# Attention feeding an MLP on one core: q and k transposed by DMA, 4-token sums on GpSimd, v loaded twice, in a new order

## The chip, the core and the metric

The kernel runs on one core of a Trainium2 chip. The metric is device time in microseconds (us) of one execution; less is better. A run is called slow when it is over 1.5% above the fastest of the same kernel. The times in us are medians of all runs; the ratios leave the slow ones out. A ratio is always the mean time of one kernel's fast runs over the mean time of the fast runs of the kernel before in the same rounds on the same chip, so it is not quite the ratio of the medians that stand beside it. The brackets after a ratio are its 95% interval.

Engines: PE is TensorE, PEld its weight load, ACT is ScalarE, DVE is VectorE, POOL is GpSimd, SP is SyncE, whose queue (SPq) issues nearly all DMA here. "The rings" are the 16 DMA engines that serve all queues.

## The reference

There are 8 batches of 8 heads, 576 tokens, 64 dimensions. Every batch does two attentions: a local one (each token sees 3 tokens to each side) and a global one over means of 4 tokens (144 of them). Their sum, as a 4608 x 512 matrix, goes through an MLP with 2048 hidden units.

```python
q_d, k_d, v_d = (t.reshape(B, H, 144, 4, D).mean(axis=3) for t in (q, k, v))
out_up    = np.repeat(softmax_attention(q_d, k_d, v_d), 4, axis=2)
out_local = softmax_attention(q, k, v, mask=np.abs(pos[:, None] - pos[None, :]) < 4)
x   = (out_up + out_local).transpose(0, 2, 1, 3).reshape(4608, 512)
h   = x @ w_in                                     # 512 x 2048
out = np.where(h > 0, h, np.exp(np.minimum(h, 0)) - 1) @ w_out    # 2048 x 512
```

Inputs and output are fp32; the kernel computes in fp16.

## The kernel before

The work on one batch is four head pairs (b, j). For each pair, q, k and v are loaded with 96 tokens on partitions (k and v with 3 halo rows to each side), cast to fp16 on GpSimd, and turned round by matmuls. QI is the identity with four-token averaging columns beside it, so the same matmul yields q transposed and its 4-token means; VR averages v.

```python
def load(b, j):                       # cut: shapes of the access patterns
    nc.sync.dma_start(out=q32[:], in_=rows(q, 0, NB, 0, QB))
    for src, dst in ((k, k32), (v, v32)):
        nc.sync.dma_start(out=dst[0:96], in_=rows(src, 0, NB, 0, QB))
        for c0, nblk, tok, p in ((lo, NB - lo, -3, 96), (0, hi, QB, 99)):
            ...                       # 2 loads of 3 halo rows each

def transposes(b, j):
    tq, tk = two("tq"), two("tk")     # PSUM
    for c in range(NB):               # q: transposed, and its 4-token means
        nc.tensor.matmul(tq[:, ...], q16[:, c, :, :], QI[:], start=True, stop=True)
    for c in range(NB):               # v: 4-token means
        nc.tensor.matmul(tq[0:KG, ...], VR[:, ...], v16[:, c, :, :], ...)
    nc.scalar.copy(out=qt[:], in_=tq[...])
    nc.vector.tensor_copy(out=vd[:], in_=tq[0:KG, ...])
    for c in range(NB):               # k, as q
        nc.tensor.matmul(tk[:, ...], k16[:, c, :, :], KI[:], start=True, stop=True)
    nc.scalar.copy(out=kt[:], in_=...); nc.vector.tensor_copy(out=kd[:], in_=...)
```

Then follow scores, exponentials, denominators ("den"), a broadcast of the reciprocals ("rd" to DRAM and "rcb" back), outputs ("lg"), and on GpSimd the sum of local and global part ("xt"), which is the MLP's input. The MLP has 9 blocks of 512 tokens: mm1 (tile hp, 16 groups of four matmuls per block), the activation, mm2 (tile op, the same count), and a store of the output (tile os). The whole order is written by hand, in "slots": one slot is one mm1 group and one mm2 group, and attention's pieces are put at slot numbers between them.

```python
SLOTS = (0, 1.6, 3.2, 4.8, 9.7, 11.3, 12.9, 14.5)     # transposes, scores of 4 pairs
base = start_of(b) - 26.5                             # start_of(b): the mm1 of block b
at(base + slots[2 * j], transposes, b, j)
at(base + slots[2 * j + 1], scores, b, j)
```

The softmax here doesn't subtract the row's maximum and nothing guards it: scores larger than these inputs give would overflow.

## Time and profile before

The median is 406.56 us (405.73 to 407.38, 2 runs). The page of the profiled run, a third one of 403.56 us, cut to the span, PE's busy time, PE and DMA in 40 slices of about 10 us (a digit is a tenth), the load queue (packets, MB, share of 16 rings' span) and the chain of waits that ended last:

```profile
span 401.8 us, 8092 instructions
...
PE 353.0 (88%) x3052; PEld 185.6 (46%) x3052; DVE 254.4 (63%) x460; ACT 203.8 (51%) x377; POOL 138.7 (35%) x184
...
PE   1465688687986899999999999999899899999996
...
DMA  6998999965966980796199639926820310100112
...
q1 hardware_dynamic: 129420, 47.62, 55.0%
...
PE 67%; DMA 12%; POOL 6%; issue 4%; DVE 4%; SPq 3%; ACTq 2%; ACT 1%; POOLq 0%; DVEq 0%
```

PE is full from the 15th slice on, and the chain is two thirds PE. The table of stretches of the same run shows for each window the length, the busy time of the engines, the granted PE clock, the share of the rings and GB/s:

```profile
core 0: us, PE busy (x) PEld busy (x) DVE busy (x) ACT busy (x) POOL busy (x), PEclk, DMA share, GB/s
...
124.00:145.00 21.00, 15.57 (x152) 8.05 (x151) 15.57 (x31) 10.04 (x18) 10.39 (x15) 0.84 0.99 188
...
165.00:203.00 38.00, 37.98 (x367) 20.21 (x366) 30.19 (x55) 24.04 (x46) 14.44 (x20) 1.00 0.67 142
203.00:241.00 38.00, 37.88 (x366) 20.07 (x365) 29.40 (x54) 23.71 (x45) 15.17 (x21) 1.00 0.74 147
```

PE is busy 37.98 of 38.00 us, at full clock.

The first denominator matmuls of a batch are a good mark for the pace. In the timeline of PE (start, length, instruction), those of batch 3 and of batch 7 stand here:

```profile
155.19 0.30 PE L240 MATMUL den<-SEED 2*32 2x288 f16 x4
...
306.08 0.30 PE L240 MATMUL den<-SEED 2*32 2x288 f16 x4
```

So four batches take 306.08 - 155.19 = 150.9 us, 37.7 us each ("the period" below is always this quarter, from batch 3 to batch 7). Each period is read from one profiled run, and single batches of a run differ; a difference of 1 us between two kernels is not clear. The time splits into a start-up of 155.2 us, a steady part of 150.9 us, and a tail of 95.7 us.

What the change is after is this piece of the timeline:

```profile
177.13 0.48 PE L171 MATMUL tq<-QI,q_2376 96*128 96x120 f16 x6
177.45 0.50 PE L176 MATMUL tq<-v_2378,VR 102*72 102x128 f16 x6
177.78 0.49 PE L186 MATMUL tk<-KI,k_2377 102*128 102x126 f16 x6
178.11 1.03 PE L368 MATMUL hp<-xt,WI 128*128 128x512 f16 x4
```

From 177.13 to 178.11 PE turns one pair round: 0.98 us, a third of it for each of q, v and k, 3.9 us per batch.

### The profile page before, as it was taken

What the parts mean: (1) busy time and instruction counts of PE and PEld (TensorE: products, weight loads), DVE (VectorE), ACT (ScalarE), POOL (GpSimd) and SP (SyncE); (2) the same over time, 40 slices, a digit from 0 to 9 for tenths busy, and PEclk for the clock granted to TensorE, in tenths of its full rate; (3) what the DMA queues carried; (4) which work ended last, traced back from release to release, by engine and by line L of the source; (5) the groups of instructions that cost most, each with busy time, mean ns of one, the idle gap of its engine ahead of it and who ended that gap; (6) DMA issues with size and microseconds to landing.
All of it is one profiled execution on the core that took longest, in us unless ns stands there. A gap on an engine that the chain in (4) does not pass through costs nothing.

```text
span 401.8 us, 8092 instructions
## 1 busy us (share of the span) xinstructions
PE 353.0 (88%) x3052; PEld 185.6 (46%) x3052; DVE 254.4 (63%) x460; ACT 203.8 (51%) x377; POOL 138.7 (35%) x184
## 2 busy tenths in 40 slices
PE   1465688687986899999999999999899899999996
PEld 1352345343553455555545554555454444444442
DVE  0134599732586797697778769886886585555510
ACT  1462157535385376747564855667375334444321
POOL 3365755460850581075028304820450050000000
PEclk9999999968999799999999999999999999999999
DMA  6998999965966980796199639926820310100112
GB/s 121 189 253 258 190 215 234 265 126 134 198 139 130 189 176 16 172 231 125 28 195 217 118 78 194 226 64 121 172 79 33 102 53 28 49 29 28 52 54 78
DMA packets 138082, 53.81 MB, mean 134 GB/s; under 512 B 122580, under 2 KB 131388, under 8 KB 138044
## 3 DMA queue, kind: packets, MB, share of 16 engines
q1 hardware_dynamic: 129420, 47.62, 55.0%
q10 hardware_dynamic: 8624, 5.68, 6.6%
q8 instruction: 24, 0.39, 0.4%
q14 instruction: 14, 0.11, 0.1%
HBM read 43.33 MB, written 9.95 MB: 133 GB/s over the span
## 4 chain that ended last, share of the span: by engine, by line
PE 67%; DMA 12%; POOL 6%; issue 4%; DVE 4%; SPq 3%; ACTq 2%; ACT 1%; POOLq 0%; DVEq 0%
PE op L388 29%; PE hp L368 25%; PE sc L204 2%; PE tk L186 2%; PE tq L176 2%; DVE e L374 2%; PE tq L171 2%; PE lg L325 2%; POOL xt L352 2%; DMA w_170<-in_moe_w_in_dram 2%; DMA rcb<-rd 2%; SPq L149 2%; ACTq L276 2%; DMA w_161<-in_moe_w_in_dram 1%; DMA w_207<-in_moe_w_out_dram 1%
## 5 line engine op out<-in xcount | busy, mean ns | idle before, releaser
L368 PE MATMUL hp<-xt,WI 128*128 128x512 f16 x576 | 150.9, 389 | 4.5 <-DVE gt L377 2.5
L388 PE MATMUL op<-WO,gt 128*128 128x512 f16 x576 | 147.7, 385 | 4.7 <-POOL WO L119 3.8
L373 ACT ACTIVATE e<-hp 128x512 f16<-128x512 f32 x144 | 85.7, 601 | 109.5 <-PE hp L368 90.8
L377 DVE SCALAR_TENSOR_TENSOR gt<-hp,e 128x512 f16<-128x512 f32 x144 | 99.6, 692 | 5.4
L374 DVE TENSOR_SCALAR e<-e 128x512 f16<-128x512 f16 x144 | 63.8, 443 | 51.5 <-ACT e L373 50.5
L368 PEld LDWEIGHTS <-WI 128*128 128x128 f16 x576 | 54.5, 99 | 71.7 <-issue 13.4
L388 PEld LDWEIGHTS <-gt 128*128 128x128 f16 x576 | 54.6, 99 | 68.8 <-issue 7.6
L232 DVE TENSOR_TENSOR mex<-pex,MASK 102x1152 f16<-102x1152 f16 x32 | 29.6, 926 | 40.3 <-ACT pex L222 40.2
L352 POOL TENSOR_TENSOR xt<-ln,gn 128x512 f16<-128x512 f16 (+7 forms) x64 | 42.0, 688 | 34.7 <-DVE ln L343 34.7
L222 ACT ACTIVATE pex<-sc 102x576 f16<-102x576 f32 x64 | 41.4, 647 | 22.3 <-PE sc L214 22.3
L182 ACT CAST qt<-tq 128x720 f16<-128x720 f32 x32 | 24.3, 760 | 30.7 <-PE tq L176 27.3
L394 ACT COPY os<-op 128x512 f32<-128x512 f32 x36 | 21.2, 588 | 25.3 <-PE op L388 25.3
L204 PE MATMUL sc<-qt,kt 64*102 64x96 f16 x384 | 19.1, 226 | 11.5 <-DVE vd L184 6.0
L184 DVE CAST vd<-tq 72x256 f16<-72x256 f32 x32 | 13.2, 413 | 22.3 <-ACT qt L182 22.3
L204 PEld LDWEIGHTS <-kt 64*102 64x102 f16 x384 | 14.4, 135 | 25.8 <-ACT kt L192 12.6
L226 ACT ACTIVATE dex<-sc 72x288 f16<-72x288 f32 x64 | 25.8, 404 | 0.0
L343 DVE TENSOR_TENSOR ln<-lg,rcb 128x576 f16<-128x576 f32 x32 | 23.9, 748 | 0.0
L192 ACT CAST kt<-tk 128x612 f16<-128x612 f32 x32 | 21.8, 680 | 0.1
L176 PEld LDWEIGHTS <-VR 102*72 102x72 f16 x192 | 14.2, 123 | 5.7 <-issue 3.9
L263 DVE RECIPROCAL rc<-den 128x288 f16<-128x288 f32 x8 | 15.6, 1949 | 1.7 <-PE den L257 1.7
L340 DVE TENSOR_TENSOR gn<-lg,rcb 128x144 f16<-128x144 f32 x32 | 9.6, 301 | 5.7 <-POOL xt L352 3.0
L194 DVE CAST kd<-tk 128x144 f16<-128x144 f32 x32 | 9.6, 300 | 1.7 <-ACT kt L192 0.5
(361 smaller groups left out, 265.7 us busy)
## 6 DMA issues: line engine op xcount, KB each, us to landing
out_dram<-os SPq DMA_DIRECT2D x36, 256.0 KB
rcb<-rd ACTq DMA_DIRECT2D x14, 288.0 KB
rcb<-rd ACTq DMA_DIRECT2D x14, 72.0 KB
w_149<-in_moe_w_in_dram SPq DMA_DIRECT2D x1, 512.0 KB
w_152<-in_moe_w_in_dram SPq DMA_DIRECT2D x1, 512.0 KB
w_155<-in_moe_w_in_dram SPq DMA_DIRECT2D x1, 512.0 KB
w_158<-in_moe_w_in_dram SPq DMA_DIRECT2D x1, 512.0 KB
w_161<-in_moe_w_in_dram SPq DMA_DIRECT2D x1, 512.0 KB
```

The lines of the kernel that those rows point to most:

```text
L182: nc.scalar.copy(out=qt[:], in_=tq[:, :, 0 : 3 * QW])
L204: nc.tensor.matmul(sc[e][0:KW, c // 3, QB * (c % 3) : QB * (c % 3) + QB], kt[r, c // 3, c % 3, :], qt[r, c // 3, QW * (c % 3) : QW * (c % ...
L222: nc.scalar.activation(out=pex[:, e, :].rearrange("p (g u) -> p g u", g=2), in_=sc[e][0:KW, :, 0:HB], func=AF.Exp, scale=SCALE,)
L226: nc.scalar.activation(out=dex[:, e], in_=sc[e][0:KG, :, HB : HB + SD], func=AF.Exp, scale=SCALE,)
L232: nc.vector.tensor_tensor(out=mex[:], in0=pex[:], in1=mk2, op=AB.mult)
L343: nc.vector.tensor_tensor(out=ln[:].rearrange("p (g u) -> p g u", g=2), in0=lg[:, :, 0:HB], in1=rcb[:, j, 0:S].rearrange("p (g u) -> p g u ...
L352: nc.gpsimd.tensor_tensor(out=xt(t)[:, j, t0 - TBLK * t : t1 - TBLK * t], in0=ln[:, a:z], in1=_rep4(gn[:, a // 4 : z // 4]), op=AB.add,)
L368: nc.tensor.matmul(hp[:], WI[:, dc, 128 * fc : 128 * fc + 128], x[:, dc, :], start=(dc == 0), stop=(dc == DMC - 1),)
L373: nc.scalar.activation(out=e[:], in_=hp[:], func=AF.Exp)
L374: nc.vector.tensor_scalar(out=e[:], in0=e[:], scalar1=1.0, scalar2=-1.0, op0=AB.min, op1=AB.add)
L377: nc.vector.scalar_tensor_tensor(out=gts[t][:, fc, :], in0=hp[:], scalar=0.0, op0=AB.max, in1=e[:], op1=AB.add)
L388: nc.tensor.matmul(op_[:], gts[t][:, fc, 128 * tt : 128 * tt + 128], WO[:, fc, :], start=(fc == 0), stop=(fc == FCN - 1),)
```

## The change

The intent is to take those 18 matmuls per pair off the full engine, in batches 2 to 7. q and k are transposed by DMA from fp16 tiles; their 4-token sums are formed on GpSimd; v is loaded a second time with 4 tokens in one partition row, so that its sums are two GpSimd additions. (Sums replace means: the exponential's scale and an indicator of 4.0 take up the factors.) With it comes a new order: batch 1's attention runs within the first mm1, every later mm1 is paired with the mm2 of the block before, and a batch's four pairs stand close together. The core of the diff:

```diff
+DMA_T = 2
+    def load_v4(b, j):                        # 288 KB, 72 rows of 4 x 1 KB
+        nc.sync.dma_start(
+            out=w32[0:KG].rearrange("p (x y) -> p x y", x=4),
+            in_=bass.AP(..., ap=[[4 * D, KG], [HB * D, 4], [1, 4 * D]]))
     def cast(b, j):
+        if b >= DMA_T:
+            cq = ck = nc.scalar.copy          # was GpSimd
+    def transposes_dma(b, j):
+        nc.sync.dma_start_transpose(out=kt[:, KP : KP + S].rearrange(...), in_=k16[:].rearrange(...))
+        nc.sync.dma_start_transpose(out=qt[:].rearrange(...), in_=q16[:].rearrange(...))
+    def sums(b, j):
+        nc.gpsimd.tensor_tensor(out=vh, in0=vh, in1=vp[:, :, :, 2:4], op=AB.add)
+        nc.gpsimd.tensor_tensor(out=vd[:]..., in0=vh[:, :, :, 0], in1=vh[:, :, :, 1], op=AB.add)
+        for src, name in ((kt[:, KP : KP + S], "kdd"), (qt[:], "qdd")):
+            nc.gpsimd.tensor_tensor(out=h[:], in0=src[:, 0:S:2], in1=src[:, 1:S:2], op=AB.add)
+            nc.gpsimd.tensor_tensor(out=d[:], in0=h[:, 0:HB:2], in1=h[:, 1:HB:2], op=AB.add)
 ...                                           # v: one load of 112 rows, no halo loads
-    SLOTS = (0, 1.6, 3.2, 4.8, 9.7, 11.3, 12.9, 14.5)
+            base, slots = 16 * (b - 2), (None, -1.5, None, 0.5, None, 2.5, None, 4.5)
+            dens, spread, outs = ((6.5, range(4)),), None, (12.5, 13.7)
+            if dma:
+                at(at_s - 5, load_v4, b, j)
+                at(at_s - 4.9, transposes_dma, b, j)
+                at(at_s - 3, sums, b, j)
 ...                                           # batches 1 and 2: reciprocals spread on PE
```

## The prediction

> **What bounds the kernel now.** From about 145 us on, TensorE: in the table of stretches PE is busy 37.98 of 38.00 us at 165:203, and nearly so at 203:241 and 241:279. One batch of attention takes a period of about 37.6 us there: 128 MLP matmuls at 0.216 us (chain: 0.86 us per four) are 27.6 us, attention is the other 10 us. Of these the transposing matmuls tq, vd and tk take 0.98 us per pair (timeline, 177.13 to 178.11), 3.9 us per batch. Before 145 us PE is not the limit: only 203 of 1152 MLP matmuls (44 us of work) are done. Loads (DMA share 0.9 to 1.2), weight casts (chain: WI and WO waits until 82 us) and the reciprocals' round trip through DRAM (chain: rd 2.1 us, rcb 6.5 us, at 122 to 132 us) set the pace, and mm2 of block 0 runs alone.
>
> **What the change does.** (1) It takes 18 matmuls per pair from PE in batches 2 to 7: 24 x 0.98 = 23.5 us, plus their PSUM copies (ACT 0.76 + 0.68, DVE 0.41 + 0.30 us per pair). (2) q and k casts go from GpSimd to ACT, about the time ACT saves. (3) GpSimd gets six sums per pair; from the xt additions (512 columns 1064 ns, 256: 629, 128: 410) I estimate 3.9 us per pair, 4.7 with the v cast; per batch about 19 plus 5.3 us of xt additions, against 15 now. (4) DMA gets 1.2 MB of v and 1.2 MB of transposes per batch on top of about 5.4 MB. The Trainium skill, "Advanced Engine Details and Errata", X-Bar Transpose, says such transposes are as fast as regular DMAs; no trace here shows one yet. (5) The instruction order shows a new schedule too: batch 1 runs inside mm1 of block 0, every later mm1 is paired with the previous mm2, batches 1 and 2 spread reciprocals on PE, halo loads vanish.
>
> **How much is critical.** Start-up: weights and batches 0 to 2 are still some 19 MB, so I expect mm2 of block 0 to wait for WO until about 85 us; then PE should fill near 90 us instead of 145. That is the larger gain. Steady: PE needs about 33.7 us per batch, but GpSimd's order is sums j0, xt, v cast, sums j1, xt: the last xt, which releases the next mm1, sits behind about 12 us of work that starts only when transposes land. I expect PE to wait 2 to 5 us per batch there: a period of 36 to 38 us, near the old one. The Trainium skill, "GPSIMD Engine Reference", Specifications, says GpSimd shares SBUF interfaces with VectorE; the trace agrees: operation e takes 0.29 us at 345:383, where GpSimd is idle, and 0.47 at 165:203. More GpSimd work means more of that.
>
> Sum: first full period ends near 121 us, five of 37, then 72 us of MLP without attention: about 378 us.
>
> **Predicted:** 378 us, 8 in 10 within 357 to 402. Faster by over 2%: 0.82; within 2%: 0.12; slower by over 2%: 0.06.
>
> **Right or wrong in the profile.** Right: hp and op alternate from about 90 us; tq and tk gone after batch 1; PE waits led by hp for POOL xt and sc for POOL kdd or qdd; GpSimd busy near 190 us; transposes land in 2 to 4 us; period 36 to 38 us.
>
> **What would make it wrong.** Transposes by DMA far slower than copies, or stuck in the one SP queue (waits of SP: loads already wait up to 12.3 us for rd): then scores stall in each batch and it loses. Or GpSimd's sums hide fully: period 34 us, total near 358.

## The result, and the profile after

The changed kernel takes 442.37 us (441.23 to 443.51, 2 runs) against 406.56: ratio 1.0881 [1.0727, 1.1035]. It is slower by 9%. The same lines of its page, and q10, ScalarE's DMA queue:

```profile
span 441.7 us, 7188 instructions
...
PE 354.0 (80%) x2644; PEld 169.5 (38%) x2644; DVE 250.5 (57%) x429; ACT 211.2 (48%) x385; POOL 198.9 (45%) x276
...
PE   2665679819878877876977798889888999999996
...
DMA  9968999786999995999399959996993030101111
...
q1 hardware_dynamic: 166924, 62.16, 74.7%
q10 hardware_dynamic: 6160, 4.06, 5.0%
...
PE 34%; POOL 27%; DMA 16%; issue 6%; SPq 5%; DVE 5%; ACT 3%; ACTq 3%; POOLq 0%; DVEq 0%
```

PE has 408 matmuls fewer, but its busy time did not fall (353.0 to 354.0 us). PE is no longer full before the tail; DMA is at 9 in most slices. In the groups of instructions the mean hp matmul grew from 389 to 402 ns, and the mean granted clock fell from 0.979 to 0.934: PE stops, and after some of the stops it runs at half speed for a few microseconds, so that such a stop costs more than its own length. The Trainium skill, "TensorE: Matmul & The Clock Gate", section "What's actually happening", says the array gets half its clock after an idle window of about 3.4 us; the trace agrees in kind, but not on the length: after the stops of 2.0 us that end at 270.90 and 315.14 us, groups of four op matmuls took 1.71 us instead of 0.86, and after one of 2.7 us that ends at 177.14 they took 0.86. The same stretches as before:

```profile
124.00:145.00 21.00, 16.37 (x144) 7.38 (x146) 12.31 (x22) 11.41 (x23) 12.81 (x20) 0.85 1.24 213
...
165.00:203.00 38.00, 31.96 (x263) 14.77 (x260) 25.89 (x41) 21.50 (x38) 22.13 (x30) 0.96 1.05 168
203.00:241.00 38.00, 29.21 (x229) 13.28 (x228) 20.79 (x36) 17.96 (x32) 17.46 (x26) 0.91 0.92 163
```

PE is busy 29 to 32 of 38 us, and the rings stand at 0.92 to 1.05 instead of 0.67 to 0.74. The marks:

```profile
165.37 0.30 PE L310 MATMUL den<-SEED 2*32 2x288 f16 x4
...
348.18 0.30 PE L310 MATMUL den<-SEED 2*32 2x288 f16 x4
```

| part of the span, us | before | after | difference |
|---|---|---|---|
| start-up, to the mark of batch 3 | 155.2 | 165.4 | +10.2 |
| batches 3 to 7 (four periods) | 150.9 (37.7 each) | 182.8 (45.7 each) | +31.9 |
| tail | 95.7 | 93.5 | -2.2 |

Inside one period, SP's timeline (start, length of issue, instruction) shows a stand and then a burst:

```profile
254.17 10.71 SPq L460 DMA_DIRECT2D out_dram<-os  x2
264.97 0.35 SPq L168 DMA_DIRECT2D vp<-in_v_dram  x1
269.33 1.21 SPq L233 DMA_TRANSPOSE kt_63<-k_3289  x1
...
284.44 2.47 SPq L233 DMA_TRANSPOSE kt_65<-k_3431  x1
```

Two output stores hold the in-order queue until 264.9; at 260 to 264 us the rings are at 0.01. Then the four pairs' loads and transposes follow each other, with the rings at 1.0 to 1.4 from 268 to 300 us. (A share over 1 means that packets overlap; 1.0 is no hard ceiling.) GpSimd's timeline shows it waiting for the second load of v and then working, with no break over 2 us, to 301.7 us (in brackets: idle before, and what ended it):

```profile
269.89 1.35 POOL L248 TENSOR_TENSOR vp<-vp 72x512 f32<-72x512 f32 x1 [14.04 <-DMA vp<-in_v_dram]
...
273.98 0.67 POOL L257 TENSOR_TENSOR hs<-kt_63 128x288 f16<-128x288 f16 x1 [1.95 <-DMA kt_63<-k_3289]
...
286.59 2.64 POOL L416 TENSOR_TENSOR xt<-ln,gn 128x192 f16<-128x192 f16 x4
```

The xt additions that the next mm1 needs stand in the middle of this run. In the waits, three lines tell who waits for what (total, times, longest):

```profile
POOL vp L248 <- DMA vp<-in_v_dram: 61.1, 7, 14.0
...
PE hp L432 <- POOL xt L416: 24.6, 15, 5.7
...
PE sc L282 <- POOL qdd L258: 12.9, 9, 2.7
```

Read alone, these lines accuse GpSimd. The experiments had to tell whether it is the cause or passes the DMA's lateness on.

### The profile page after: what moved, and what is told of

Read it like the earlier page. It is cut to its first block, busy times and chain, and to the rows that moved or that the text cites. A ratio compares the mean times of both kernels' runs of the same rounds, so it can differ in the third digit from the quotient of the medians.

```text
span 441.7 us, 7188 instructions
## 1 busy us (share of the span) xinstructions
PE 354.0 (80%) x2644; PEld 169.5 (38%) x2644; DVE 250.5 (57%) x429; ACT 211.2 (48%) x385; POOL 198.9 (45%) x276
## 3 DMA queue, kind: packets, MB, share of 16 engines
q1 hardware_dynamic: 166924, 62.16, 74.7%
## 4 chain that ended last, share of the span: by engine, by line
PE 34%; POOL 27%; DMA 16%; issue 6%; SPq 5%; DVE 5%; ACT 3%; ACTq 3%; POOLq 0%; DVEq 0%
PE op L452 17%; PE hp L432 15%; POOL xt L416 7%; POOL hs L257 5%; POOL vp L248 4%; POOL vd L249 3%; ACTq L342 3%; POOL kdd L258 2%; DMA vp<-in_v_dram 2%; ACT e L437 2%; DMA w_350<-in_moe_w_in_dram 2%; POOL qdd L258 2%; DMA w_569<-in_moe_w_out_dram 2%; DVE ln L406 2%; DMA w_368<-in_moe_w_in_dram 2%
## 5 line engine op out<-in xcount | busy, mean ns | idle before, releaser
L432 PE MATMUL hp<-xt,WI 128*128 128x512 f16 x576 | 161.8, 402 | 36.0 <-POOL xt L416 24.6
L452 PEld LDWEIGHTS <-gt 128*128 128x128 f16 x576 | 54.9, 101 | 69.5 <-issue 10.7
L248 POOL TENSOR_TENSOR vp<-vp 72x512 f32<-72x512 f32 x24 | 30.6, 1275 | 61.1 <-DMA vp<-in_v_dram 61.1
L416 POOL TENSOR_TENSOR xt<-ln,gn 128x448 f16<-128x448 f16 (+7 forms) x60 | 40.2, 699 | 26.4 <-DVE ln L406 26.4
L249 POOL TENSOR_TENSOR vd<-vp 72x256 f16<-72x256 f32 x24 | 19.9, 831 | 1.9
L282 PE MATMUL sc<-qdd,kdd 64*72 64x144 f16 x96 | 8.1, 245 | 13.2 <-POOL qdd L258 12.9
L328 DVE RECIPROCAL rc<-den 128x288 f16<-128x288 f32 (+1 forms) x9 | 17.6, 1951 | 1.1 <-PE den L310 0.9
L257 POOL TENSOR_TENSOR hs<-qtd 128x288 f16<-128x288 f16 x24 | 16.1, 670 | 1.9
L258 POOL TENSOR_TENSOR kdd<-hs 128x144 f16<-128x144 f16 x24 | 13.6, 567 | 1.9
L258 POOL TENSOR_TENSOR qdd<-hs 128x144 f16<-128x144 f16 x24 | 10.8, 451 | 1.9
L394 PE MATMUL lg<-dex,vd 72*64 72x144 f16 x128 | 10.8, 252 | 0.0
```

Source lines behind the costliest of these rows:

```text
L248: nc.gpsimd.tensor_tensor(out=vh, in0=vh, in1=vp[:, :, :, 2:4], op=AB.add)
L249: nc.gpsimd.tensor_tensor(out=vd[:].rearrange("p g (e d) -> p e g d", e=2), in0=vh[:, :, :, 0], in1=vh[:, :, :, 1], op=AB.add,)
L257: nc.gpsimd.tensor_tensor(out=h[:], in0=src[:, 0:S:2], in1=src[:, 1:S:2], op=AB.add)
L258: nc.gpsimd.tensor_tensor(out=d[:], in0=h[:, 0:HB:2], in1=h[:, 1:HB:2], op=AB.add)
L416: eng.tensor_tensor(out=xt(t)[:, j, t0 - TBLK * t : t1 - TBLK * t], in0=ln[:, a:z], in1=_rep4(gn[:, a // 4 : z // 4]), op=AB.add,)
L432: nc.tensor.matmul(hp[:], WI[:, dc, 128 * fc : 128 * fc + 128], x[:, dc, :], start=(dc == 0), stop=(dc == DMC - 1),)
```

## The experiments

Four theories. **A**: GpSimd's serial run of sums, casts and xt. **B**: the added DMA: it takes time on rings that were not idle in this stage. **C**: ScalarE, which issues the reciprocals' DMAs and stands while it does. **D**: order: the queue stands at output stores while the rings are idle, and the pairs are packed. A further suspect is the transpose itself, slower than a copy. All experiments passed the comparison with the reference. "The changed kernel" below is always the one of the last section: 1.0881, period 45.7.

### e1: all transposes on PE, in the new order

```diff
-DMA_T = 2
+DMA_T = 8
-... (None, -1.5, None, 0.5, None, 2.5, None, 4.5); dens 6.5; outs (12.5, 13.7)
+... (-1.7, -0.5, 0.3, 1.5, 2.3, 3.5, 4.3, 5.5); dens 7.0; outs (12.8, 14.0)
```

> The new schedule, but q and k transposed on PE in all eight batches (no DMA transposes, no GpSimd sums, no second load of v). If the DMA-transpose path (any part of it) is what made the changed kernel slow: the period from one batch's denominators to the next falls from 44 to 47 us to about 38, total 390 to 410 us. If the new schedule itself is at fault: total stays at 430 us or more.

Measured: 419.03 us against 402.0, ratio 1.0407 [1.026, 1.0554]; period 41.0 us, mark of batch 3 at 159.0 us. The new order alone, without any DMA transpose, GpSimd sum or second load, is 4% slower than the kernel before, and its start-up is not shorter (159.0 against 155.2). So less than half of the loss belongs to the order; the DMA path adds the rest: 45.7 - 41.0 = 4.7 us per batch, although it takes 3.9 us per batch off PE.

### e2, e3: doses

e2 adds one GpSimd addition of 128 x 512 per pair; e3 one more 288 KB load of the same rows of v per pair, from batch 3 on, that nobody reads.

```diff
+        nc.gpsimd.tensor_tensor(out=dz[:], in0=qt[:, 0:512], in1=qt[:, 64:576], op=AB.add)   # e2
+        if b > DMA_T:                                                                       # e3
+            nc.sync.dma_start(out=dv[0:KG]..., in_=...)      # as load_v4
```

> The changed kernel with one more GpSimd addition of about 1.06 us per pair (24 in all, result unused). Theory A (GpSimd's serial run of sums is in the loop that sets the period): all of it shows, 4 us per batch, total +20 to +26 us. Theory B (DMA traffic sets the pace) and theory C (ScalarE blocked by issuing rcb DMAs and casts): +0 to +4 us.

> The changed kernel with one more load of 288 KB per pair from batch 3 on (20 loads, 5.9 MB, result unused). Theory B (DMA traffic): about 5.9 MB at 200 GB/s, total +20 to +30 us. Theory A (GpSimd's chain): only a later arrival of the first v tile of a batch, +0 to +8 us. Theory C: no change.

Measured: e2 453.55 us, ratio 1.1264 [1.1104, 1.1424], period 47.8: 2.1 us more per batch for 4.6 us more work (27.8 us for 24 pairs). e3 472.56 us, ratio 1.1736 [1.1543, 1.1929], period 51.5: 5.8 us more per batch for 1.2 MB. By the page, the queue's share times the span is 0.758 x 468.6 = 355 us of ring time against 0.747 x 441.7 = 330 us: 25 us more in five batches, 5 us each. The dose of DMA costs all of its ring time, that of GpSimd about half of its work. Doses show that both lie on the way; they do not say which one binds.

### e4: the sums of q and k on VectorE

```diff
-            nc.gpsimd.tensor_tensor(out=h[:], ...)   # and the next line
+            nc.vector.tensor_tensor(out=h[:], ...)
```

> The changed kernel with the four sums of k and q per pair on VectorE; the two sums of v stay on GpSimd. Theory A: GpSimd's run per batch shrinks by 4 x 2.2 us, the period falls from about 45 to 37 to 40 us, total 400 to 420 us. Theories B and C: within 5 us of the changed kernel (442 us).

Measured: 447.99 us, ratio 1.1126 [1.0983, 1.1269], period 46.3. GpSimd's busy time fell from 198.9 to 146.3 us, 8.8 us per batch, and nothing was gained. The chain of waits by line shows what stands there now:

```profile
PE op L452 20%; PE hp L432 18%; DMA kt<-k 10%; DVE hs L257 4%; DMA w<-in_moe_w_out_dram 4%; DMA w<-in_moe_w_in_dram 4%; ACTq L342 3%; DMA k<-in_k_dram 2%; ACT e L437 2%; DVE gt L441 2%; DVE ln L406 2%; PE sc L274 2%; POOL xt L416 2%; DVE kdd L258 2%; DVE e L438 1%
```

The landing of the k transposes, which does not occur in the changed kernel's chain, has 10% of the span. Theory A alone does not explain the loss. That GpSimd passed the lateness on is the likely reading, but not a proof: the sums went to VectorE, which now has 13% of the chain instead of 5%.

### e5, e6: ScalarE's DMA issues, and everything earlier

e5 spreads the reciprocals on PE in every batch, so ScalarE issues no DMA. e6 puts casts, second load, transposes and loads 3 slots earlier from batch 3 on, and the sums 1.5 slots, with one more buffer of nearly everything.

```diff
-            dens, spread, outs = ((6.5, range(4)),), None, (12.5, 13.7)
+            dens, spread, outs = ((6.5, range(4)),), (8.3, 9.1), (12.5, 13.7)      # e5
-                at(at_s - 5, load_v4, b, j)          # and four more lines like it
+                at(at_s - 5 - early, load_v4, b, j)  # e6: early = 3 if b >= 3
```

> The changed kernel with the reciprocals of every batch spread on PE, as the first three batches have it: no rd and rcb DMAs (0.8 MB per batch) and no 2.6 us of ScalarE issuing them. Theory B (DMA time): period falls by about 4 us, from 45.7 to 41 to 42. Theory C (ScalarE blocked): about the same, 3 to 4 us, but then PE no longer stands still just before the lg matmuls. Theory A (GpSimd): no change in the period, total a little longer by 1.2 us of PE per batch.

> The changed kernel with casts, second v load, DMA transposes and loads of batches 3 to 7 placed 3 slots earlier in program order, sums 1.5 slots earlier; same work, same bytes, one more buffer of k, q and the sums. Theory D (one in-order queue leaves the DMA rings idle for 8 to 9 us per batch while it waits for an output tile): idle time shrinks, period 45.7 to 38 to 42 us, total 15 to 35 us less. Theory B in its pure form (DMA rings simply full): period stays within 1.5 us.

Measured: e5 444.19 us, ratio 1.0986 [1.0809, 1.1163], period 45.6; e6 448.71 us, ratio 1.1098 [1.0948, 1.1248], period 46.1. Neither gains, and issuing earlier did not help. Theory C finds no support. But e5 is a miss for theory B as well. It took the reciprocals' DMA, about 0.8 MB per batch, off the rings: its page has no line for q10. The rings' mean share from the mark of batch 3 to that of batch 7 fell from 0.94 to 0.79, and theory B had expected a period of 41 to 42 us. In exchange PE, which was not full, got 1.2 us of work per batch, by the estimate in the expectation.

### e7: the sums of v on PE, no second load

```diff
-                at(at_s - 5, load_v4, b, j)
-        nc.gpsimd.tensor_tensor(out=vh, ...); nc.gpsimd.tensor_tensor(out=vd[:]..., ...)
+        for c in range(NB):
+            nc.tensor.matmul(vps[0:KG, ...], VR[:, ...], v16[:, c, :, :], ...)
+        nc.vector.tensor_copy(out=vd[:], in_=vps[0:KG, 0:256]...)
```

> The changed kernel with the sums of v made on PE from the fp16 tile as before: no second load of v (1.2 MB per batch, about 5 us of the rings' time), no v sums on GpSimd (8.4 us per batch), 1.3 us more of PE. e4_kq_sums_dve took as much from GpSimd and gained nothing. Theory B: period falls by 4 to 6 us. Theory A: it falls by more than in e4, but only with GpSimd gone from the chain. If neither, within 1 us.

Measured: 423.96 us against 404.79, ratio 1.0486 [1.0351, 1.0621], period 41.95. PE does six matmuls per pair more than in the changed kernel, and the period is 3.75 us shorter. The v part is the bulk of what the DMA path costs: e7 is close to e1 (1.0407) although q and k still go through DMA and GpSimd.

### e8: plain copies instead of transposes

```diff
-        nc.sync.dma_start_transpose(out=kt..., in_=k16...)    # and q
+            nc.sync.dma_start(out=dst[0:96], in_=flat[:, 0:S])
+            nc.sync.dma_start(out=dst[96:128], in_=flat[0:32, 192 : 192 + S])
```

> Wrong result on purpose: each DMA transpose is replaced by plain copies of the same bytes from the same tile to the same tile. I estimate from the queue's time in e1, e3 and the changed kernel that a DMA transpose of 147 KB takes 1.46 us of all 16 rings (101 GB/s) where plain loads run at 209 GB/s. If that extra price matters: period falls by 4 to 7 us, total 20 to 35 us less. If bytes or order alone matter: within 5 us of the changed kernel.

Measured: 438.79 us, ratio 1.0852 [1.0687, 1.1018], period 44.7. The kernel is wrong on purpose; the comparison with the reference passed it all the same, so on these data (q and k drawn with a deviation of 0.1) that comparison says little about q and k. The bytes are the same 62.16 MB. The ring time falls from 330 us to 0.689 x 435.5 = 300 us, the packets from 166,924 to 145,420. So transposing costs 30 us of ring time more than copying the same bytes, 0.6 us for each of the 48, yet the period gains 1.0 us only, and the ratios' intervals overlap. A part of the 30 us may be the size of the packets: in the packet records the transposes move 256 bytes in each, as the loads of q, k and v do, the copies 1152. The Trainium skill, "Advanced Engine Details and Errata", section "X-Bar Transpose (TRN2)", says that such transposes are as fast as regular DMAs: in ring time this does not agree, but the difference is not the main cause here.

### e9, e10: the second load alone, the sums of v alone

Both start from e7. e9 gives back the second load, which nobody reads; e10 gives back the two GpSimd additions, on a tile of zeros, unused.

```diff
+                at(at_s - 5, load_v4, b, j)                                      # e9
+        nc.gpsimd.tensor_tensor(out=vh, in0=vh, in1=zeros..., op=AB.add)         # e10, and
+        nc.gpsimd.tensor_tensor(out=vd2[:]..., in0=vh[...], in1=vh[...], op=AB.add)
```

> The run that formed the v sums on TensorE and took away both the second load of v and its GpSimd sums had a period of 41.95 us per batch against 45.7 of the changed kernel. This run gives back the second load alone: it lands in its buffer and nobody reads it. If the rings' time is what costs (theory B), the period goes back to about 45 us (45 to 46.5) and the ratio to about 1.08. If it is the GpSimd work or the wait for the landing (theory A), it stays at about 42 (41.5 to 43), ratio about 1.05.

> The twin of the last: no second load of v, but the two GpSimd additions of it are made per pair, on a tile of zeros, and their result is not used (the v sums that are used come from TensorE). Theory A (GpSimd's serial run): period back to 44 to 46 us, ratio about 1.08. Theory B (ring time): stays at 41.5 to 43 us, ratio about 1.05. If both twins rise by about 2 us, the cost is shared.

Measured: e9 442.67 us against 403.35, ratio 1.0947 [1.0869, 1.1026], period 45.3; e10 429.53 us, ratio 1.0641 [1.0603, 1.0679], period 43.8. The load that nobody reads brings back 3.4 of the 3.75 us; the sums 1.9, with a ratio whose interval just overlaps that of e7. (They do not add up.) In e9 nothing waits for the load itself. What it delays shows in the waits of e7, then of e9:

```profile
POOL hs L259 <- DMA kt<-k: 39.5, 7, 15.2
```

```profile
POOL hs L259 <- DMA kt<-k: 98.5, 15, 18.1
```

GpSimd's wait for the k transposes grows from 39.5 to 98.5 us. Not all of this is new: the waits of the same instructions that are put down to PE fall from 47.4 to 18.7 us, so together they grow by 30 us. The load delays the transposes.

### e15: the same unused load, last in the queue

```diff
-                at(at_s - 5, load_v4, b, j)       # ahead of the pair's transposes
+                at(at_s - 2.8, load_v4, b, j)     # after them and after the next loads
```

> The unused second load of v alone raised the packed order with v sums on TensorE from 41.95 to 45.3 us per batch. Here the same load of the same bytes stands after the pair's transposes and after the next loads in the queue, instead of right ahead of the k transpose. If its volume costs (ring time), the period stays at 44 to 46 us. If its place costs, because it delays the k transpose by its 4.9 us, the period falls back to 42 to 43 us.

Measured: 437.94 us against 405.48, ratio 1.0834 [1.0773, 1.0895], period 44.4. By the periods, 0.9 of the 3.4 us come from the load's place ahead of the k transpose (the ratios' intervals overlap, so even that is not certain), and 2.5 stay wherever it stands. What costs is mostly that the load is made, not where it stands.

### e12, e13, e14: the old, spread places

From batch 4 on, the four pairs stand where the kernel before has them: two pairs early, two late, over 18 slots. e12 does it to e1 (with eight buffers instead of seven for what waits for the outputs), e13 to the whole change, e14 to e7.

```diff
+            if b >= 4:
+                slots = (-10.5, -8.9, -7.3, -5.7, -0.8, 0.8, 2.4, 4.0)   # e13, e14: scores only
+                dens, outs = ((5.6, range(4)),), (12.0, 13.6)
```

> The run with all transposes on TensorE in the new schedule had a period of 41.0 us, against 37.6 of the kernel before. This one has, from batch 4 on, the places in the order that the kernel before uses (two pairs 26.5 slots ahead of the mm1 that needs them, two pairs 17 slots ahead; eight buffers instead of seven). If the packing of the four pairs into seven slots is what costs in the new schedule, the period from batch 4 on falls to 37.5 to 38.5 us, and the ratio to about 1.00 to 1.02. If the cost lies in what else is new (k copies into one long tile, pairing of mm1 with the previous mm2), it stays near 41 us, ratio 1.03 to 1.04.

> The changed kernel whole, with DMA transposes, GpSimd sums and second load of v, but from batch 4 on with the places in the order of the kernel before (four pairs spread over 18 slots). With all transposes on TensorE that spreading took the period from 41.0 to 37.3 us. If the steady loss of the changed kernel is mainly the packing of the pairs, its period falls from 45.7 to below 39 us, ratio about 1.03. If the DMA path costs its own share, as theory B says (it added 4.7 us per batch to the packed order), the period stays at 41 to 44 us, ratio 1.05 to 1.08.

> The same spread places, with the v sums on TensorE and no second load: what is left of the change is q and k by DMA transpose and their sums on GpSimd. If those two are harmless by themselves, the period is under 37.3 us, as TensorE has 0.65 us per pair less to do (35 to 37.3), ratio 0.99 to 1.02, the best of the versions in the new schedule. If the DMA transposes cost by themselves, it is over 38.5 us, ratio over 1.03.

| order | all on PE | q, k by DMA; v on PE | the whole change |
|---|---|---|---|
| packed: ratio (period, us) | e1 1.0407 (41.0) | e7 1.0486 (41.9) | 1.0881 (45.7) |
| spread: ratio (period, us) | e12 1.0270 (37.3) | e14 1.0329 (39.4) | e13 1.0778 (43.6) |

The times are 414.52 us (e12), 436.21 (e13) and 418.03 (e14). The intervals of the spread row are 1.0233 to 1.0307, 1.0274 to 1.0384 and 1.0719 to 1.0836. In e12 the period is that of the kernel before, and PE is full again, at 37.71 of 38 us with the rings at 0.79:

```profile
205.00:243.00 38.00, 37.71 (x371) 20.30 (x369) 30.92 (x55) 23.54 (x46) 15.18 (x21) 1.00 0.79 150
```

So the steady loss of the new order was mainly the packing. The extra buffer is not what did it alone: e13 and e14 keep seven, and gain 2.1 and 2.6 us over their packed twins. From batch 4 to batch 7, where all batches stand in the spread places, the periods are 37.3 (e12), 39.8 (e14) and 43.9 us (e13). The start-up stays the worse one: in e12 the mark of batch 3 comes at 168.3 us instead of 155.2 (159.0 in e1), so that most of the gain is lost again and the intervals of e1 and e12 overlap. The transposes of one pair of batch 4 now stand ahead of that mark; the rest of the delay is not explained. In e14 PE is no longer full, and in the period shown here the rings are near 1 (0.79 on the mean from the mark of batch 3 to that of batch 7, 0.64 in e12):

```profile
203.00:241.00 38.00, 33.77 (x294) 16.57 (x283) 25.16 (x47) 22.08 (x42) 15.35 (x25) 1.00 0.95 164
```

The DMA path therefore loses in the spread order too: 2.1 us per batch for q and k, and another 4.2 us for v. e14's forecast of at most 37.3 us missed.

### e11, e16, e18: attempts at a version that beats both

e11 and e16 take the kernel before, in its own order, and give it only the v part (second load, sums on GpSimd). In e11 the load is issued one pair ahead, in e16 three pairs ahead and from pair 10 on. e18 is the kernel before with the reciprocals of batches 1 and 2 spread on PE and the stores three slots later.

```diff
+                at(base + slots[2 * j] - 0.05, load_v4, *pairs[n + 1])   # e11
+                at(base + slots[2 * j], load_v4, *pairs[n + 3])          # e16
+                at(base + (slots[2 * j - 2] if j else -3.1) + 0.2, sums_v, b, j)
-        if b == 0:
+        if b <= 2:
             at(base + d0 + 1, spread_pe, b, 0)                           # e18
```

> A candidate to beat both: the kernel before in its own order, with only the v part of the change: from batch 2 on v is loaded a second time in groups of 4 tokens and summed on GpSimd, so six matmuls per pair (a third of the 0.98 us of transposing per pair) and one VectorE copy go. TensorE is full there and queue time is at 55% of the span, so I expect 1.3 us per batch less on TensorE, period about 36.5 us, total 397 to 402 us where the kernel before takes 406, ratio about 0.98. If the ring time hurts here too, although the rings have room on average, the period stays at 37.6 or rises, ratio 1.00 to 1.03.

> The candidate again, mended: the kernel before with the second load of v three pairs ahead, beside the other loads of its pair, instead of one pair ahead, from pair 10 on. The first candidate lost 18% with GpSimd waiting 149 us for vp to land. If that was the place of the load in the queue alone, GpSimd's wait for vp is under 15 us now, the period is 36.3 to 37.5 us and the ratio 0.98 to 1.00. If the bytes themselves cost, the period is 39 us or more, ratio over 1.03.

> Candidate to beat both: the kernel before, with the reciprocals of batches 1 and 2 spread on TensorE, as in batch 0, instead of the round trip through DRAM, and stores three slots later. At 122 to 132 us the chain of the kernel before runs through that round trip (rd 2.1, rcb 6.5 us) while TensorE has no other work, and loads wait for rd up to 12.3 us. If that stretch is what the start-up waits for, 4 to 12 us go before 155 us, the steady period stays at 37.5, and the ratio is 0.97 to 0.99. If loads set the pace of the start-up, nothing changes: 0.995 to 1.005.

Measured: e11 475.96 us, ratio 1.1792 [1.1753, 1.1831]; e16 448.73 us, ratio 1.1079 [1.1016, 1.1143]; e18 409.39 us, ratio 1.0162 [1.0126, 1.0198]. All three miss, and no version beats the kernel before. e16 is instructive. Its period is 45.8 us; these are two stretches of 4 us in one period:

```profile
260.00:264.00 4.00, 4.00 (x59) 2.28 (x56) 3.76 (x5) 2.25 (x4) 0.00 (x0) 1.00 0.00 0
...
284.00:288.00 4.00, 0.41 (x5) 0.44 (x6) 1.23 (x4) 0.00 (x0) 3.92 (x7) 0.71 0.98 175
```

The rings do nothing at 260 us, and 20 us later PE starves while they are full. In that run no DMA was issued by SP between 255 and 266.81 us; the load that ends the stand is released by the landing of rd, with which it shares no data (the release is inferred from semaphores, and what orders the two was not tested). GpSimd waits 92.7 us in all for the first loads of v, but only 9.8 for the second, for which e11 had waited 149.3: the forecast of this wait (under 15 us) held, and the period got no shorter for it than 45.8. The kernel before has the same kind of idle stretch (0.02 at 268 to 272 us) and gets away with it, presumably because its burst is shorter; no run shows that. In e18 two edits went in together, so it cannot be told which of them lost the 1.6%; its mark of batch 3 comes at 163.1 us instead of 155.2 and its period is 37.6, so the loss lies in the start-up. e11's period is 48.9 us.

### e17: stores later in the queue

```diff
-            nc.sync.dma_start(out=out[r : r + 128, :], in_=os_[:])
+            late.append((r, os_))
+        if part == 2 or (t, i) == (NT - 1, 15):   # three slots later
+            while late: ...                        # the same store
```

> The changed kernel whole, with one edit: each output store stands three slots later in the queue's order, when its tile has long been copied, so that the queue no longer stands still at a store (in the changed kernel it waited 133.7 us, 21 times, for the copies of ACT). Theory B2: the period is an idle stretch of the rings, in which the one in-order queue stands at stores, plus a burst that the rings' rate bounds; then the queue's wait for os falls below 20 us, loads spread, and the period falls from 45.7 to 41 to 43.5 us, ratio 1.04 to 1.07. If the stores' waits cost nothing, because the loads behind them are held by buffers or by the casts anyway (the transposes wait for ACT too, 29 us), the wait moves to those lines and the period stays at 45 to 46.5, ratio 1.08 to 1.10.

Measured: 445.85 us against 403.84, ratio 1.1097 [1.1028, 1.1167] (plain means of the three fast runs here and of the eight of the kernel before give 1.104), period 46.0. SP's waits, of the changed kernel and then of e17:

```profile
SPq L460 <- ACT os L458: 133.7, 21, 9.6
SPq L233 <- ACT e L437: 29.4, 11, 5.0
```

```profile
SPq L464 <- ACT os L458: 98.7, 16, 9.4
SPq L233 <- ACT e L437: 56.4, 11, 13.7
```

The wait at the stores falls by 35 us and comes back, 27 us of it, at the k transposes (L233), which wait for their casts on ScalarE. The forecast had counted on a wait under 20 us at the stores; 98.7 us are left, so e17 is only half a test. Where the stand got shorter, something else in this one in-order queue held the next item. Theory D is right about packing; that the stores' place in the queue costs time is not shown.

### What the runs settle

Where a load or a store stands in the queue made little difference in the changed kernel's order: e6 and e17 gained nothing, e15 0.9 us. (In the old order e16 has a period 3.0 us shorter than e11, but it also has the load for fewer pairs.) Every added load of v, read or not, cost time (e3, e9, e15, and with its sums e11 and e16), and taking it and its sums away gained 3.75 us (e7). The new order costs 3.7 us of the period by its packing (e1, e12).

It does not follow that the rings' time binds the changed kernel. The ring time of the queue, share times span, is 0.553 x 416.1 = 230 us in e1, 0.675 x 421.8 = 285 us in e7, and 330 us in the changed kernel: 55 us more with the transposes of 7.1 MB and 45 us more with the second load of v, also 7.1 MB, in six batches. An estimate from these numbers: the kernel before has the rings at 0.67 to 0.74 of a period of 37.7 us, 25 to 28 us; with 55 / 6 = 9.2 us and 45 / 6 = 7.5 us that is 42 to 45 us per batch, just under the measured period of 45.7. But the rings' share from the mark of batch 3 to that of batch 7 does not go with the period:

| | before | e1 | e7 | e16 | e5 | e8 | e17 | changed | e9 |
|---|---|---|---|---|---|---|---|---|---|
| rings' share | 0.65 | 0.61 | 0.80 | 0.65 | 0.79 | 0.83 | 0.84 | 0.94 | 0.96 |
| ring time per batch, us | 24.5 | 25.0 | 33.6 | 29.8 | 36.0 | 37.1 | 38.6 | 43.0 | 43.5 |
| period, us | 37.7 | 41.0 | 41.95 | 45.8 | 45.6 | 44.7 | 46.0 | 45.7 | 45.3 |

e5 and e8 have 7.0 and 5.9 us less ring time per batch than the changed kernel and gain 0.1 and 1.0 us. e7 and e5 have nearly the same share, and 3.7 us lie between their periods. Nor is ring time a fixed price: in the packet records the second load's own packets take 27 of the 45 us, and the rest is other packets taking longer. So the runs show which parts of the change cost time: the packing, the second load of v and, less surely, GpSimd's additions (e2 and e10 lose 2.1 and 1.9 us), which do not simply add up. Through which link of the loop of queue, transposes, GpSimd and buffers the load costs its 3.4 us stays open, and so does why e16, with only 24 us more ring time in its load queue than the kernel before (0.549 x 446.3 = 245 against 0.550 x 401.8 = 221), loses 8 us per batch.

## Why the prediction was wrong, point by point

1. *PE bounds the kernel from 145 us.* Right: e12 came back to a period of 37.3 us with PE full.
2. *23.5 us of matmuls go.* Right as work, worthless as time: PE's busy time is 354.0 us, because the array stops more often and runs at a clock of 0.934.
3. *GpSimd's sums cost an estimated 3.9 us per pair, and PE waits 2 to 5 us per batch for xt.* The size was nearly right: the groups of vp, vd, hs, kdd and qdd sum up to 107 us for 24 pairs, 4.5 us each, and GpSimd's busy time, forecast near 190 us, was 198.9. PE's waits for xt and qdd are 24.6 + 12.9 = 37.5 us, 6 per batch. But the mechanism was incomplete: taking 8.8 us per batch off GpSimd (e4) gained nothing.
4. *"DMA gets 1.2 MB of v and 1.2 MB of transposes per batch on top of about 5.4 MB."* This is the step that failed. The prediction listed these bytes and gave them no time: its period is made of PE's work and GpSimd's alone. It cited the Trainium skill's statement that transposes are as fast as regular DMAs, but even regular DMAs were not free: the second load of v alone, which nobody reads, costs 3.4 us per batch (e9 against e7), the whole DMA path 4.7 us net of what PE saves (the changed kernel against e1). The predicted 36 to 38 us became 45.7. In ring time the rings had room for 10 to 12 us per batch, at 0.67 to 0.74 of 37.7 us, and the change asks for an estimated 9.2 + 7.5 = 16.7; but as e5 shows, this sum is not the mechanism. The forecast that transposes land in 2 to 4 us was short in part: from the issue at 269.33 to GpSimd's start on the tile at 273.98 it is 4.65 us in the quoted period, and in e7 the median from issue to landing is 4.6 us for k and 2.8 for q.
5. *Start-up: PE full near 90 us instead of 145, "the larger gain".* This step failed too. The prediction's own sum puts the mark of batch 3 near 136 us (an estimate: 121 us and 6.5 of 16 slots of a 37 us period); it came at 165.4, 10 us later than before. These 29 us and four periods longer by 8.7 us make up the 64 us between 378 and 442. The mm2 of block 0 was forecast for about 85 us and began at 99.5 (at 72.5 in the kernel before), and by 145 us 184 MLP matmuls were done, in the kernel before 203. The rings are at 1.24 from 124 to 145 us (0.99 before), but the added bytes are not the whole of it: e1, without them, has done 204 by 145 us and reaches the mark at 159.0. Why the new order starts no faster was not tested.
6. *The new order as a neutral carrier.* The prediction described it and never asked what packing four pairs into seven slots does. In the period it costs 41.0 - 37.3 = 3.7 us per batch (e1, e12).
7. *"What would make it wrong: transposes far slower than copies, or stuck in the one SP queue."* It looked in the right quarter, the DMA, but e8 shows that transposing as such is worth 1 us per batch, and e15 that the load's place in the queue is worth 0.9 us. The waits of the SP queue are long (133.7 us at stores), but no run shows what they cost: e17 removed a quarter of them and gained nothing.

## What to carry to other kernels

Before moving work from a full engine to DMA, read the rings' share in that very stage, not the queue's share of the span, turn the added transfers into ring time, and see whether the sum stays well under the period. That is a first check and not enough: e16 lost with the rings at 0.65. When one engine's wait is named, relieve that engine in a run of its own: if the time does not move, its work alone is not the cause (and look at where the work went). Test a new order separately from the mechanism that comes with it, since here the order alone took nearly half of what was lost.

## What the Trainium skill lacked or had wrong

- "Advanced Engine Details and Errata", X-Bar Transpose (TRN2): "TRN2 transpose DMAs are as fast as regular DMAs". For SBUF tiles of 96 x 768 in fp16, 48 transposes took 30 us of ring time more than plain copies of the same bytes, with 21,504 packets more (e8); the copies moved larger packets, so how much is due to the transposing is open.
- "DMA: Bandwidth & Descriptors", "Issuing engines are not separate DMA queues", says that all DMAs run on the same 16 engines whoever starts them. What it lacks is the case here: one queue in program order, standing 10.7 us at two stores, leaves those engines at 0.01 and then at 1.0 to 1.4 in the same period; and shortening the one stand (e17) moved part of it to the next item.
- "DMA: Bandwidth & Descriptors", "Why a DMA increments its semaphore by 16 and not by 1", says that a transfer is spread over the largest number of engines, up to 16, that divides its slowest dimension. For the second load of v, 72 rows, that gives 12, for the 96 and 112 rows of the others 16. The trace's packet records fit it, weakly: of this load at most 15 to 19 packets are in flight at once, of the weight loads of 128 rows with the same packet size 19 to 23. No run here changed the row count, so how much of the load's cost is due to it is open; it is the next thing to try.
